# Instance normalisation on one core: mixed PE and bn_stats batches, 4-tile first loads, and small parameter loads moved to another queue

## Chip, cores, metric

One core of one Trainium2 chip runs the whole kernel. The metric is device time in microseconds (us), median of several executions; lower is better. Each execution carries a state, fast or slow. Verdicts use fast runs alone and call a difference under 2% "same". Wherever a ratio is given, it is the mean time of one kernel's fast runs over the mean of the other's fast runs of the same rounds, so it is not quite the ratio of the medians that are quoted.

## The reference

```python
B, C, H, W = 32, 576, 16, 32            # x, g, b in bfloat16
def reference(x, g, b):
    mu = x.mean(axis=(-2, -1), keepdims=True)
    var = ((x - mu) * (x - mu)).mean(axis=(-2, -1), keepdims=True)
    xhat = (x - mu) / jnp.sqrt(var + 1e-5)
    return xhat * g.reshape(1, -1, 1, 1) + b.reshape(1, -1, 1, 1)
```

There are 32 x 576 = 18,432 instances of 512 elements. The kernel lays them out as 144 tiles of 128 instances (one per partition). In bfloat16 that is 18.87 MB in and as much out. Every tile must be read once, have its mean and variance taken, and then be rewritten in place as scale * x + bias.

## The kernel before

A small list scheduler in Python places all the work when the program is built. All 144 tiles stay in SBUF (`xt`), so the sync queue issues all loads first, then the stores as tiles are finished. A tile's statistics come in one of two ways:

- a "D" tile: one `bn_stats` on DVE;
- a "P" tile: PE multiplies by -1/512 times the identity and so folds 512 elements into 64 partial sums, DVE reduces them to the mean, and ACT squares (x - mean) with an accumulated sum.

Tiles are grouped in batches. At the end of a batch a handful of tiny DVE and ACT instructions turn the statistics of all its tiles into `scale` and `bias`. Then "applies", one per tile, run on ACT or POOL, whichever is free.

```python
# [cut: cost table]
head = [("D", 2), ("P", 2), ("D", 4), ("P", 3), ("D", 8), ("P", 5)]   # a batch is all D or all P
tail = [("D", 6), ("P", 3), ("D", 4)]                                 # between them 14 D, 8 P, ...
# [cut: load_chunks: 2, 2, 4 tiles, then 8 tiles each]
@block.sync
def _(sp):
    em = _Emit(sp, None, "SP")
    for ci, (a, e_) in enumerate(load_chunks):
        if ci == plan["gb_after"]:                                    # after the second load
            sp.dma_start(gb4[:, 0, :], g_src).then_inc(sGB, 16)
            sp.dma_start(gb4[:, 1, :], b_src).then_inc(sGB, 16)
        sp.dma_start(xt[:, a:e_, :], xr[:, a:e_, :]).then_inc(ld_sems[ci], 16)
    for s_ in stores:
        dep_waits(em, [("ap", n) for n in range(s_["t0"], s_["t1"])])
        sp.dma_start(outr[:, s_["t0"]:s_["t1"], :], xt[:, s_["t0"]:s_["t1"], :]).then_inc(sST, 16)
    sp.wait_ge(sST, 16 * len(stores))
# [cut: the other engines run the streams that the scheduler made]
```

Of the kernel before, what the change touches and what calls it, by code (L numbers as in the profile page):

```python
# [2 lines left out]

# [12 lines left out]
EPS = 1e-5  # L16

COST = dict(
    bn=593.0,
    sq=704.0,  # L20
    mm=240.0,
    mm_fixed=150.0,
    ap_A=705.0,
    ap_G=744.0,
    ap_V=325.0,
    small=90.0,
    small_per_elem=1.05,
    rd_fixed=130.0,
    rd_per_tile=67.0,
    sqrt=110.0,  # L30
    lat=130.0,
    tile_dma=306.0,
    dma_start=1050.0,
    dma_fixed=40.0,
    dma_issue=450.0,
# [3 lines left out]
class _Task:  # L39
    __slots__ = ("key", "eng", "dur", "deps", "cls", "order", "batch", "start", "end", "idx", "ready", "idx_sq")  # L40

    def __init__(self, key, eng, dur, deps, cls, order, batch=None):
        self.key = key
        self.eng = eng
        self.dur = dur
        self.deps = deps
        self.cls = cls
        self.order = order
        self.batch = batch
        self.start = None  # L50
        self.end = None
        self.idx = None
        self.ready = None


def _default_pattern(nt):
    if nt < 24:
        pat = []
        left = nt
        typ = "D"  # L60
        while left > 0:
            s = min(left, 3 if typ == "D" else 2)
            pat.append((typ, s))
            left -= s
            typ = "P" if typ == "D" else "D"
        return pat
    head = [("D", 2), ("P", 2), ("D", 4), ("P", 3), ("D", 8), ("P", 5)]
    tail = [("D", 6), ("P", 3), ("D", 4)]
    used = sum(s for _, s in head) + sum(s for _, s in tail)
    mid = []  # L70
    left = nt - used
    typ = "D"
    while left > 0:
        s = 14 if typ == "D" else 8
        s = min(s, left)
        mid.append((typ, s))
        left -= s
        typ = "P" if typ == "D" else "D"
    return head + mid + tail


def build_plan(nt, pattern=None, load_chunks=None, cost=None, store_max=8, store_big=16, store_tail=4,
               use_pool=True, use_pe=True):
# [5 lines left out]
    if not use_pe:  # L89
        pattern = [("D", s) for _, s in pattern]  # L90
    assert sum(s for _, s in pattern) == nt, (pattern, nt)
    batches = []
    t0 = 0
    for typ, s in pattern:
        assert typ in ("D", "P")
        if typ == "P":
            assert s <= 8, "P batch must fit one PSUM bank (8 tiles)"
        batches.append(dict(typ=typ, t0=t0, t1=t0 + s, idx=len(batches)))
        t0 += s
    tile_batch = [None] * nt  # L100
    for b in batches:
        for n in range(b["t0"], b["t1"]):
            tile_batch[n] = b["idx"]

    if load_chunks is None:
        load_chunks = []
        sizes = [2, 2, 4]
        pos = 0
        for s in sizes:
            if pos + s <= nt:  # L110
                load_chunks.append((pos, pos + s))
                pos += s
        while pos < nt:
            s = min(8, nt - pos)
            load_chunks.append((pos, pos + s))
            pos += s
    assert load_chunks[0][0] == 0 and load_chunks[-1][1] == nt
    tile_chunk = [None] * nt
    arrive = []
    t = c["dma_start"]  # L120
    n_issue = 0
    gb_after = min(2, len(load_chunks))
    for ci, (a, b_) in enumerate(load_chunks):
        if ci == gb_after:
            n_issue += 2
            t += 100.0
        t = max(t, n_issue * c["dma_issue"] + c["dma_start"])
        n_issue += 1
        t += (b_ - a) * c["tile_dma"] + c["dma_fixed"]
        arrive.append(t)  # L130
        for n in range(a, b_):
            tile_chunk[n] = ci
    gb_arrive = (gb_after + 2) * c["dma_issue"] + c["dma_start"] + 400.0
# [11 lines left out]
    add(("SQ0",), "A", 1400.0, [("DS",)], -1)  # L145
    add(("I0",), "G", 350.0, [], -1)
    add(("I0s",), "G", 200.0, [], -1)
    add(("I1",), "V", 100.0, [("I0",)], -1)
    add(("I1s",), "V", 100.0, [("I0s",)], -1)
    add(("GB",), "T", 300.0, [("I1s",), ("gbld",)], -1)  # L150

    psum_banks = 4
    p_batches = [b for b in batches if b["typ"] == "P"]
    for k, b in enumerate(p_batches):
        b["bank"] = k % psum_banks
        b["pk"] = k
    junk_n = 4
    sq_list = []
    for b in batches:
        bi = b["idx"]  # L160
        w = b["t1"] - b["t0"]
        sm = c["small"] + c["small_per_elem"] * w
        if b["typ"] == "D":
            for n in range(b["t0"], b["t1"]):
                add(("bn", n), "V", c["bn"], [("ld", tile_chunk[n])], 10, bi)
            last_bn = [("bn", n) for n in range(b["t0"], b["t1"])]
            add(("R1", bi), "V", sm, last_bn, 1, bi)
            add(("R2a", bi), "V", sm, last_bn, 1, bi)
            add(("R2b", bi), "V", sm, last_bn, 1, bi)
            add(("T2", bi), "V", sm, [("R2a", bi), ("R2b", bi)], 1, bi)  # L170
            add(("V", bi), "V", sm, [("T2", bi), ("R1", bi)], 1, bi)
            add(("C1", bi), "A", c["sqrt"], [("V", bi)], 0, bi)
            ms_dep = ("R1", bi)
        else:
            deps = [("ld", ci) for ci in sorted(set(tile_chunk[n] for n in range(b["t0"], b["t1"])))] + [("I1",)]
            if b["pk"] >= psum_banks:
                deps.append(("Rd", p_batches[b["pk"] - psum_banks]["idx"]))
            add(("mm", bi), "T", c["mm_fixed"] + c["mm"] * w, deps, 10, bi)
            add(("Rd", bi), "V", c["rd_fixed"] + c["rd_per_tile"] * w, [("mm", bi)], 1, bi)
            add(("Cp", bi), "V", sm, [("Rd", bi)], 2, bi)  # L180
            for n in range(b["t0"], b["t1"]):
                deps = [("Rd", bi)]
                if len(sq_list) >= junk_n:
                    deps.append(("sq", sq_list[-junk_n]))
                tsq = add(("sq", n), "A", c["sq"], deps, 10, bi)
                tsq.idx_sq = len(sq_list)
                sq_list.append(n)
            add(("C1", bi), "A", c["sqrt"], [("sq", n) for n in range(b["t0"], b["t1"])], 0, bi)
            ms_dep = ("Cp", bi)
        add(("C2", bi), "V", sm + 25, [("C1", bi)], 0, bi)  # L190
        add(("C3", bi), "V", sm, [("C2", bi), ("GB",)], 0, bi)
        add(("C4", bi), "V", sm, [("C3", bi), ms_dep], 0, bi)
        add(("C5", bi), "V", sm, [("C4", bi), ("GB",)], 0, bi)
# [22 lines left out]
    ap_dur = dict(A=c["ap_A"], G=c["ap_G"], V=c["ap_V"])  # L216
    v_drain = [False]
    g_stop = [False]
# [17 lines left out]
    def pick(eng, t):  # L236
# [15 lines left out]
        if soon is not None and eng in ("V", "A"):  # L252
            starving = ap_backlog(t) <= 2
            if starving and soon - t <= 450.0:
# [3 lines left out]
        can_apply = (eng == "A") or (eng == "G" and use_pool and not g_stop[0]) or (eng == "V" and not pending["V"])  # L258
# [8 lines left out]
    while n_left > 0:  # L267
        guard += 1
        assert guard < 200000, "scheduler stuck"
        progressed = False  # L270
        for eng in sorted(engines, key=lambda e: free[e]):
# [7 lines left out]
            if tk.key[0] == "ap":  # L279
                ap_pending.remove(tk)  # L280
                tk.eng = eng
                tk.dur = ap_dur[eng]
                if eng == "V":
                    g_stop[0] = True
# [28 lines left out]
    while a < nt:  # L313
# [5 lines left out]
        else:  # L319
            sz = store_big if ap_end[min(nt - 1, a + store_big - 1)] < arrive[-1] else store_max  # L320
# [5 lines left out]
    tq = arrive[-1]  # L326
    slack = []
    for s in stores:
        slack.append(tq - (s["ready"] + 600.0))
        tq = max(tq, s["ready"] + 600.0) + (s["t1"] - s["t0"]) * c["tile_dma"] + c["dma_fixed"]  # L330
    makespan = max(tk.end for tk in tasks.values())
    return dict(
        nt=nt, batches=batches, load_chunks=load_chunks, stores=stores, tasks=tasks, streams=streams,
        tile_batch=tile_batch, tile_chunk=tile_chunk, makespan=makespan, est_total=tq + 2000.0,
        junk_n=junk_n, psum_banks=psum_banks, cost=c, use_pool=use_pool, gb_after=gb_after,
        store_slack=slack,
    )


def plan_summary(plan):  # L340
# [9 lines left out]
    lines.append(f"  compute makespan {plan['makespan']/1e3:.1f}us  est total {plan['est_total']/1e3:.1f}us")  # L350
# [22 lines left out]
def bass_standalone__instancenorm__sampling_kernel(  # L373
# [26 lines left out]
    have_p = any(bb["typ"] == "P" for bb in batches)  # L400
# [6 lines left out]
    with nc.Block() as block, contextlib.ExitStack() as es:  # L407
# [11 lines left out]
        rstd_sb = sb("rstd_sb", [P, NT], F32)  # L419
        t_sb = sb("t_sb", [P, NT], F32)  # L420
        st = sb("st", [P, NT, 6], F32)
        d_sb = sb("d_sb", [P, NT], F32)
        q_sb = sb("q_sb", [P, NT], F32)
        v_sb = sb("v_sb", [P, NT], F32)
        std_sb = sb("std_sb", [P, NT], F32)
        nm_sb = sb("nm_sb", [P, NT], F32)
# [8 lines left out]
        assert NT * 2 + NT <= 512 and 3 * NT <= 512  # L435
        MA_ps = ps[:, 4, 0:2 * NT].rearrange("p (n j) -> p n j", j=2)
        d_ps = ps[:, 4, 2 * NT:3 * NT]
        nm_ps = ps[:, 5, 0:NT]
# [4 lines left out]
        HALF = float(F // 4)  # L443

        def dep_waits(em, deps):
            need = {}
            for d in deps:
                if d[0] == "ld":
                    sem, val = ld_sems[d[1]], 16
                elif d[0] == "gbld":  # L450
                    sem, val = sGB, 32
                else:
                    pt = tasks[d]
                    sem, val = sem_of[pt.eng], pt.idx + 1
# [170 lines left out]
```

## Time and profile before

| | before |
|---|---|
| median, first 4 runs | 96.58 us (96.28 to 96.64) |
| span of the profiled run | 94.8 us |
| bytes moved | 37.79 MB |
| DVE / ACT / POOL busy | 82% / 79% / 73% |
| batches | 19 |

The first view is the page of the kernel before. In the rows of 40, each column is a slice of 2.37 us; DMA is the busy share in tenths and GB/s what moved in that slice. The last line is the summary, by engine, of the chain of work that ended last.

```profile
span 94.8 us, 749 instructions
...
DMA  1899999999999999999999999999999999779996
GB/s 35 240 379 425 425 425 429 432 415 429 415 422 425 411 429 425 418 425 422 415 467 436 415 415 415 429 453 429 404 429 422 418 436 425 321 297 442 404 401 245
...
q1 hardware_dynamic: 5200, 37.75, 96.2%
...
ACT 53%; DMA 20%; SPq 6%; issue 5%; DVE 4%; PE 4%; DVEq 1%
...
```

What to see: the DMA row is full (9) almost everywhere, at 404 to 467 GB/s. Less moves in the first three slices (35, 240, 379), in slices 35 and 36 (321, 297), and in the last. The chain names ACT for 53%. That is the chain of compute; it matters only where a store is late because of it.

The second view gives the same kernel in stretches: from:to in us, length, busy time of each engine with its number of instructions, granted PE clock, DMA share, GB/s.

```profile
...
core 0: us, PE busy (x) PEld busy (x) DVE busy (x) ACT busy (x) POOL busy (x), PEclk, DMA share, GB/s
...
3.50:4.00 0.50, 0.00 (x0) 0.00 (x0) 0.36 (x1) 0.00 (x0) 0.00 (x0) 1.00 0.96 156
4.00:4.50 0.50, 0.24 (x3) 0.24 (x4) 0.50 (x2) 0.00 (x0) 0.00 (x0) 1.00 0.45 57
4.50:5.00 0.50, 0.50 (x8) 0.50 (x5) 0.47 (x2) 0.00 (x0) 0.00 (x0) 1.00 0.75 229
60.00:70.00 10.00, 0.00 (x0) 0.00 (x0) 10.00 (x28) 10.00 (x16) 10.00 (x14) 0.50 1.01 427
...
82.00:83.00 1.00, 0.00 (x0) 0.00 (x0) 1.00 (x4) 1.00 (x3) 1.00 (x3) 0.50 0.45 188
83.00:84.00 1.00, 0.00 (x0) 0.00 (x0) 1.00 (x10) 1.00 (x4) 1.00 (x2) 0.50 0.41 172
84.00:85.00 1.00, 0.00 (x0) 0.00 (x0) 0.42 (x4) 1.00 (x3) 1.00 (x2) 0.50 0.95 401
...
```

Two holes: 3.5 to 5 us (156, 57, 229 GB/s) and 82 to 84 us (188, 172). The steady rate is 427. The waits of the sync queue after 78 us say what the second hole was waiting for, and the timeline shows how late the last coefficients come (start, length, instruction):

```profile
...
engine line waited for: us in total, times, longest us
SPq L370 <- POOL xt L555: 6.0, 2, 4.2
...
```

```profile
...
84.54 2.91 ACT L552 ACTIVATE xt<-xt,bias_sb,scale_sb 128x512 bf16<-128x512 bf16 x4
...
85.28 0.16 DVE L534 TENSOR_TENSOR bias_sb<-ps,t_sb 128x4 f32<-128x4 f32 x1
...
```

The store queue waited once for 4.2 us for an apply of POOL. The last `bias` is written at 85.3 us, and ACT begins its last four applies at 84.5 us.

### The profile page before, as it was taken

Reading aid. Unit: us, or ns where it says so; the run is one execution under the profiler, and the core shown is the slowest. Engines: PE = TensorE matmul, PEld = TensorE weight load, DVE = VectorE, ACT = ScalarE, POOL = GpSimd, SP = SyncE. Lnnn points to the kernel's source line nnn. Section 1 sums busy time; section 2 is a strip of 40 time slices with the busy share of each in tenths; the row PEclk is TensorE's granted clock in tenths of the full one; section 3 lists DMA queues with packets and bytes.
Section 4 is the critical chain, followed back from the end, with each engine's and each line's share of the span. In section 5 each row is a group of like instructions: output and inputs, shape, how many; then the busy total and the mean of one; then the engine's idle time right before and its main releaser. Section 6 shows DMA issues by size and latency. Waiting matters only on the chain.

```text
span 94.8 us, 749 instructions
## 1 busy us (share of the span) xinstructions
PE 23.1 (24%) x74; PEld 9.2 (10%) x74; DVE 77.3 (82%) x245; ACT 75.1 (79%) x171; POOL 68.8 (73%) x96
## 2 busy tenths in 40 slices
PE   0230554039129209494087000000000000000000
PEld 0210431013013003030044000000000000000000
DVE  2445687997899999999899998999999988979000
ACT  6062575959699499999999999999999999999000
POOL 3000600989992399999999999999999999995000
PEclk9999999999999999999955555555555555555555
DMA  1899999999999999999999999999999999779996
GB/s 35 240 379 425 425 425 429 432 415 429 415 422 425 411 429 425 418 425 422 415 467 436 415 415 415 429 453 429 404 429 422 418 436 425 321 297 442 404 401 245
DMA packets 5204, 37.79 MB, mean 399 GB/s; under 512 B 592, under 2 KB 592, under 8 KB 1232
## 3 DMA queue, kind: packets, MB, share of 16 engines
q1 hardware_dynamic: 5200, 37.75, 96.2%
q14 instruction: 4, 0.03, 0.1%
HBM read 18.88 MB, written 18.87 MB: 398 GB/s over the span
## 4 chain that ended last, share of the span: by engine, by line
ACT 53%; DMA 20%; SPq 6%; issue 5%; DVE 4%; PE 4%; DVEq 1%
ACT xt L552 29%; ACT junk L538 22%; DMA xt<-in_x_dram 20%; SPq L574 5%; PE ps L547 4%; DVE xt L555 2%; ACT std_sb L518 1%; DVE nm_sb L512 1%; DVEq L407 1%; DVE rstd_sb L521 0%; SPq L572 0%; DVE t_sb L529 0%; DVE scale_sb L524 0%; DVE bias_sb L534 0%; SPq L573 0%
## 5 line engine op out<-in xcount | busy, mean ns | idle before, releaser
L555 POOL TENSOR_SCALAR xt<-xt,scale_sb,bias_sb 128x512 bf16<-128x512 bf16 x90 | 67.9, 781 | 17.3 <-DVE bias_sb L534 8.9
L491 DVE BATCH_NORM_STATS2 st<-xt 128x6 f32<-128x512 bf16 x94 | 60.0, 679 | 4.0 <-DMA xt<-in_x_dram 4.0
L538 ACT ACTIVATE junk<-xt,nm_sb 128x512 bf16<-128x512 bf16 x50 | 35.4, 710 | 8.3 <-DVE nm_sb L512 8.3
L552 ACT ACTIVATE xt<-xt,bias_sb,scale_sb 128x512 bf16<-128x512 bf16 x50 | 36.6, 803 | 2.2 <-DVE bias_sb L534 2.1
L547 PE MATMUL ps<-xt,ident 128*128 128x512 bf16 (+3 forms) x72 | 22.8, 496 | 28.5 <-DMA xt<-in_x_dram 16.7
L547 PEld LDWEIGHTS ps<-xt,ident 128*128 128x128 bf16 x72 | 9.0, 139 | 41.9 <-issue 26.7
L538 ACT ACTIVATION_READ_ACCUMULATOR junk<-xt,nm_sb 128x1 f32 x50 | 9.5, 189 | 0.0
L512 DVE TENSOR_REDUCE nm_sb<-ps 128x8 f32<-128x512 f32 (+3 forms) x9 | 4.6, 514 | 2.3 <-PE ps L547 2.1
L521 DVE RECIPROCAL rstd_sb<-std_sb 128x8 f32<-128x8 f32 (+6 forms) x19 | 3.7, 194 | 2.1 <-ACT std_sb L518 2.1
L518 ACT ACTIVATE std_sb<-v_sb 128x8 f32<-128x8 f32 (+6 forms) x19 | 3.7, 199 | 1.2 <-DVE v_sb L506 1.1
L534 DVE TENSOR_TENSOR bias_sb<-ps,t_sb 128x8 f32<-128x8 f32 (+6 forms) x19 | 2.9, 158 | 0.2
L524 DVE TENSOR_TENSOR scale_sb<-ps,rstd_sb 128x8 f32<-128x8 f32 (+6 forms) x19 | 2.9, 156 | 0.2
L555 DVE TENSOR_SCALAR xt<-xt,scale_sb,bias_sb 128x512 bf16<-128x512 bf16 x4 | 2.2, 598 | 0.0
L494 DVE TENSOR_REDUCE ps<-st 128x28 f32<-128x56 f32 (+4 forms) x10 | 1.9, 189 | 0.1
L488 ACT ACT_TABLE_LOAD x1 | 1.3, 1283 | 0.7 <-PEq L610 0.7
L529 DVE SCALAR_TENSOR_TENSOR t_sb<-ps,scale_sb 128x14 f32<-128x14 f32 (+4 forms) x10 | 1.6, 162 | 0.2
L500 DVE TENSOR_REDUCE ps<-st 128x14 f32<-128x28 f32 (+4 forms) x10 | 1.8, 175 | 0.0
L497 DVE TENSOR_REDUCE d_sb<-st 128x14 f32<-128x28 f32 (+4 forms) x10 | 1.7, 168 | 0.0
L503 DVE SCALAR_TENSOR_TENSOR q_sb<-d_sb,ps 128x14 f32<-128x14 f32 (+4 forms) x10 | 1.5, 153 | 0.0
L506 DVE TENSOR_TENSOR v_sb<-q_sb,ps 128x14 f32<-128x14 f32 (+4 forms) x10 | 1.5, 151 | 0.0
L515 DVE COPY ps<-nm_sb 128x8 f32<-128x8 f32 (+3 forms) x9 | 1.4, 160 | 0.0
L531 DVE TENSOR_TENSOR t_sb<-ps,scale_sb 128x8 f32<-128x8 f32 (+3 forms) x9 | 1.3, 149 | 0.1
(14 smaller groups left out, 2.9 us busy)
## 6 DMA issues: line engine op xcount, KB each, us to landing
xt<-in_x_dram SPq DMA_DIRECT2D x17, 1024.0 KB, 22.5
out_dram<-xt SPq DMA_DIRECT2D x11, 1024.0 KB, 6.5
out_dram<-xt SPq DMA_DIRECT2D x3, 2048.0 KB, 17.6
out_dram<-xt SPq DMA_DIRECT2D x2, 512.0 KB, 6.0
xt<-in_x_dram SPq DMA_DIRECT2D x2, 256.0 KB, 3.0
xt<-in_x_dram SPq DMA_DIRECT2D x1, 512.0 KB, 5.6
gb<-in_g_dram SPq DMA_DIRECT2D x1, 1.1 KB
gb<-in_b_dram SPq DMA_DIRECT2D x1, 1.1 KB
```

The source lines that it names most:

```text
L491: ins = e.bn_stats(st[:, n, :], xt[:, n, :])
L494: ins = e.tensor_reduce(MA_ps[:, t0:t1, :], st_pairs(t0, t1 - t0, 1, 2), AX.X, ALU.add)
L512: ins = e.tensor_reduce(nm_sb[:, t0:t1], src, AX.X, ALU.add)
L518: ins = e.activation(std_sb[:, t0:t1], v_sb[:, t0:t1], ACTF.Sqrt, bias=EPS, scale=1.0 / F)
L521: ins = e.reciprocal(rstd_sb[:, t0:t1], std_sb[:, t0:t1])
L524: ins = e.tensor_tensor(scale_sb[:, t0:t1], g_ps[:, t0:t1], rstd_sb[:, t0:t1], ALU.mult)
L534: ins = e.tensor_tensor(bias_sb[:, t0:t1], b_ps[:, t0:t1], t_sb[:, t0:t1], ALU.add)
L538: ins = e.activation(junk[:, j, :], xt[:, n, :], ACTF.Square, bias=nm_sb[:, n:n + 1], scale=1.0, accum_out=v_sb[:, n:n + 1])
L547: ins = e.matmul(dst, ident[:], xt[:, t0:t1, j * NP_:(j + 1) * NP_], start=(j == 0), stop=(j == JB - 1), skip_group_check=True)
L552: ins = e.activation(xt[:, n, :], xt[:, n, :], ACTF.Identity, bias=bias_sb[:, n:n + 1], scale=scale_sb[:, n:n + 1])
L555: ins = e.tensor_scalar(xt[:, n, :], xt[:, n, :], scale_sb[:, n:n + 1], bias_sb[:, n:n + 1], ALU.mult, ALU.add)
L574: sp.dma_start(xt[:, a:e_, :], xr[:, a:e_, :]).then_inc(ld_sems[ci], 16)
```

## The change

The intent is to bring the kernel nearer to its DMA limit. Batches become mixed: each has some P and some D tiles and one set of coefficient instructions, so there are 7 batches instead of 19. The first loads are 4 tiles instead of 2. The loads of g and b (1.1 KB each) move from the sync queue to ACT's queue. The last applies no longer go to DVE. The scheduler's cost table is set anew, and a factor of 2 or 4 moves between the statistics instructions so that both kinds of tile share one set.

```diff
+_TUNED_PATTERNS = {
+    144: [(5, 9), (7, 7), (12, 14), (8, 15), (10, 19), (4, 16), (2, 16)],   # (P tiles, D tiles) per batch
+}
-    head = [("D", 2), ("P", 2), ("D", 4), ("P", 3), ("D", 8), ("P", 5)]
-    tail = [("D", 6), ("P", 3), ("D", 4)]
...
-        sizes = [2, 2, 4]
+        load_sizes = [4, 4] + [8] * ((nt - 8) // 8 + 1)
...
         @block.sync
             for ci, (a, e_) in enumerate(load_chunks):
-                if ci == plan["gb_after"]:
-                    sp.dma_start(gb4[:, 0, :], g_src).then_inc(sGB, 16)
-                    sp.dma_start(gb4[:, 1, :], b_src).then_inc(sGB, 16)
                 sp.dma_start(xt[:, a:e_, :], xr[:, a:e_, :]).then_inc(ld_sems[ci], 16)
...
         @block.scalar
+            a.dma_start(gb4[:, 0, :], g_src).then_inc(sGB, 16)
+            a.dma_start(gb4[:, 1, :], b_src).then_inc(sGB, 16)
...  (cost table, coefficient arithmetic and bookkeeping of waits left out)
```

## The prediction

> What bounds it now. The DMA engines. The page gives 37.79 MB for a 94.8 us span; in the slices from 7 us to 80 us they are 90% busy or more and move about 425 GB/s. The Trainium skill ("DMA: Bandwidth & Descriptors", Bandwidth) measured 425 GB/s for one core's 16 MB copy; this trace agrees, so I take 425 as the ceiling. 37.75 MB at 425 GB/s is 88.8 us. First bytes move at 1.8 us and the span ends 1 us after the last byte, so the floor is near 91.6 us; 3.2 us are lost. The stretches of the trace show where:
> - Start: between 3.5 and 5.0 us the rate falls to 156, 57, 229 GB/s. The sync queue issued two 256 KB loads, then the tiny g and b loads (0.37 and 0.26 us), then the next. To 10 us 1.5 us is missing, some of it ramp.
> - 82 to 84 us: 188 and 172 GB/s, about 1.15 us lost. The last store queue waited for POOL's applies (one wait of 4.2 us): the tail batches' coefficients came late, and DVE has no slack after 40 us.
> - After 84 us the rate is about 405, some 0.4 us.
> The chain of waits names ACT 53%, but ACT matters only where it makes a store late.
>
> What changes. (1) First loads 512 KB instead of 256 KB; g and b move to ACT's queue, so x loads are issued about 0.43 us apart with nothing between. (2) 19 batches (10 by bn_stats, 9 by PE) become 7 mixed ones: 96 bn_stats (was 94), 48 squares (was 50). Small DVE instructions fall from about 150 to 70; at 0.10 us each DVE saves about 7 us. PE reductions, 0.64 us for 8 tiles, are 10 instead of 9. (3) The applies: POOL 92 (was 90), ACT 52 (50), DVE none (4). The new scheduler costs only reorder.
>
> Timeline by hand from trace paces (bn 0.597, square 0.704, ACT apply 0.704, POOL apply 0.755 us): first load lands about 4.2, second 5.5, third 8.0. The first batch now needs 9 bn up to tile 13, so first coefficients come near 14.5 us (was 9.2). POOL then runs nearly without gaps: 92 x 0.755 = 69.5, ending near 84 to 86 (was 86.7). DVE: 57 bn + 4.6 PE reductions + 8 small + 2.5 waits from 5.5 gives last coefficients near 78 to 79 (was 85.4). The last 18 tiles are split 9 and 9, ready near 85.8. DMA by then has moved only about 35.8 of 37.75 MB, so stores are queued ahead: no starvation in the tail, slack of 2 to 3 us. First stores need only be ready at 46 us.
>
> So: start saves about 1.0 to 1.3, the dip at 82 to 84 saves 1.1, the tail 0.2 to 0.5; together near 2.8.
>
> Predicted: 93.8 us, 8 in 10 between 93.0 and 95.2; faster by over 2% 0.80, within 2% 0.18, slower 0.02.
>
> To check: no slice under 400 GB/s between 5 and 88 us; no fall at 3.5 to 5 us; POOL first apply near 14.5 us, last coefficients near 79, last apply near 86; DVE idle grows; the chain ends in DMA, not ACT.
>
> What would make it wrong: the fall at 3.5 us is ramp or latency of the queue, not the g and b loads (then 94.8); a batch boundary leaves POOL and ACT idle and the stores starve mid-way (95 or more); stores drain slower than 425 at the end.

## The result, and the profile after

The changed kernel took 95.01 us (median of 11 runs, 94.79 to 95.22), the kernel before 96.35 us (median of 16). The ratio is 0.985 (95% interval 0.9824 to 0.9875): within 2%, though clearly faster. Executions over 1.5% slower than the fastest of the same kernel are left out of the means. The time lies inside the predicted range, near its slow end. The gain is half of the 2.8 us that was forecast, and the likeliest class (faster by over 2%, at 0.80) did not come.

The page of the changed kernel, the same lines (a slice is now 2.32 us):

```profile
span 92.8 us, 678 instructions
...
DMA  2999999999999999999999999999999999999993
GB/s 34 362 445 420 431 424 424 424 424 420 427 413 424 416 424 420 424 416 427 409 455 452 431 424 395 431 427 424 420 431 431 427 427 431 424 424 427 434 406 152
...
q1 hardware_dynamic: 5184, 37.75, 97.5%
...
POOL 74%; DVE 7%; DMA 5%; PE 2%; POOLq 1%; issue 0%; SPq 0%
...
```

The same stretches of the changed kernel:

```profile
...
core 0: us, PE busy (x) PEld busy (x) DVE busy (x) ACT busy (x) POOL busy (x), PEclk, DMA share, GB/s
...
3.50:4.00 0.50, 0.00 (x0) 0.00 (x0) 0.00 (x0) 0.00 (x0) 0.00 (x0) 1.00 1.11 437
4.00:4.50 0.50, 0.00 (x0) 0.00 (x0) 0.00 (x0) 0.00 (x0) 0.00 (x0) 1.00 1.01 418
4.50:5.00 0.50, 0.40 (x2) 0.13 (x2) 0.00 (x0) 0.00 (x0) 0.00 (x0) 1.00 1.11 459
60.00:70.00 10.00, 0.00 (x0) 0.00 (x0) 10.00 (x26) 10.00 (x16) 10.00 (x14) 0.50 1.01 426
...
82.00:83.00 1.00, 0.00 (x0) 0.00 (x0) 0.00 (x0) 1.00 (x3) 1.00 (x2) 0.50 1.01 426
83.00:84.00 1.00, 0.00 (x0) 0.00 (x0) 0.00 (x0) 0.52 (x1) 0.99 (x2) 0.50 1.01 426
84.00:85.00 1.00, 0.00 (x0) 0.00 (x0) 0.00 (x0) 0.00 (x0) 0.00 (x0) 0.50 0.99 418
...
```

Both holes are gone. From the third slice on, the queue runs at 409 to 455 GB/s, with one slice at 395, until the last two (406, 152). Compute has become early: the timelines below give the last `bias` and the last ACT applies, then POOL's applies.

```profile
...
75.68 7.84 ACT L593 ACTIVATE xt<-xt,bias_sb,scale_sb 128x512 bf16<-128x512 bf16 x11
...
76.40 0.18 DVE L577 TENSOR_TENSOR bias_sb<-ps,t_sb 128x18 f32<-128x18 f32 x1
```

```profile
...
14.72 69.27 POOL L596 TENSOR_SCALAR xt<-xt,scale_sb,bias_sb 128x512 bf16<-128x512 bf16 x92 [13.21 <-DVE bias_sb L577]
```

The last coefficients come at 76.4 us (85.3 before), ACT's last applies end at 83.5 and POOL's at 84.0 us, and POOL runs 92 applies without a gap. After 84 us only the queue works, for 8 us. So nearly everything that the prediction asked of the profile is there. The question is why it buys only half. One check needs a warning: I had said that the chain would end in DMA. The page's chain says POOL 74%. That chain follows the last piece of compute; experiment 1 shows that the time does not depend on it.

### A finer reading: the completions of one transfer

On the sync queue, the changed kernel has 576 packets of 4 bytes for its 36 loads and stores, 16 for each. The Trainium skill ("DMA: Bandwidth & Descriptors", Why a DMA increments its semaphore by 16 and not by 1) says that a DMA runs on up to 16 engines that finish independently, and that each posts its own increment after its data. So the 16 four-byte packets of the last store show when each of the 16 DMA engines was done. That each comes from another engine is the page's statement; the trace agrees in the count. The packed records do not name the engine of a packet, so which engine is late cannot be read here. In the table, times are from the first data packet (about 1.7 us into the span), counted from the packet records of each profiled execution; "mean" is over the 16. Where the engines lie further apart than the last store takes (1.25 us), the last 16 packets can hold two of one engine; in the rows from a 1.6 us spread up this sets the mean up to 0.13 us too late.

```
profiled run   time    mean of 16  last of 16  last - first  time - last
before         96.60     92.18       92.28        0.18          4.32
after          94.88     89.70       90.38        1.07          4.50
a_nowait       95.15     89.79       90.68        1.25          4.47
a_gb_late      95.23     89.76       90.72        1.29          4.51
a_oldstart     96.05     90.58       91.53        1.32          4.52
a_gb_sp        95.89     90.52       91.37        1.39          4.52
b_nowait       96.23     90.66       91.96        1.81          4.27
b_newstart     96.12     91.67       91.77        0.18          4.35
b_gb_act       96.45     92.05       92.14        0.17          4.31
a_bigst        95.37     89.84       90.88        1.62          4.49
a_big          95.34     89.44       90.81        1.70          4.53
a_pe6          95.99     90.05       91.31        1.94          4.68
a_pad          96.18     89.90       91.69        2.46          4.49
```

The first two rows account for the result. The average DMA engine finished 2.48 us earlier (92.18 - 89.70), close to the 2.8 predicted. The last one finished only 1.90 us earlier (92.28 - 90.38), because the engines now finish 1.07 us apart instead of 0.18. Another 0.18 us went between the last completion and the end of the time (4.50 against 4.32). 2.48 - 0.58 - 0.18 = 1.72 us, which is 96.60 - 94.88. In all 13 rows the time follows the last engine, by 4.27 to 4.68 us.

Following the spread from transfer to transfer shows where it comes from. In the kernel before, the completions of one transfer were about 2.0 us apart from the third load (7.6 us) on, stayed so until the store that ended at 84.0 us, and were 0.16 us apart at the next one: the hole at 82 to 84 us is where the engines that were ahead ran dry and waited, while the late ones worked off their queue. The last completion of the transfer before the hole came at 83.97 us of the span and that of the next at 86.44, 2.47 us later. One engine's share of such a transfer is 8 packets of 309 ns, 2.47 us: the latest engine had no idle time to lose in that hole. In the changed kernel they were 0.47 us apart from 5 to 25 us, 1.08 at the load ending at 28.1 us, and stayed at 1.07 to the end, since nothing made the early engines wait.

That leads to the theory and its rivals:

- Theory A: the changed kernel is bound by the queue of its latest DMA engine; in the kernel before, the latest engine's queue and the end of compute were two bounds of nearly equal length, so the hole at 82 to 84 us cost almost nothing.
- Rival B: the hole was a plain loss of 1.1 us (the prediction), and something else in the changed kernel, a compute wait, takes it back.
- Rival C: the gain comes from one part of the change alone, the start or the batches.

### The profile page after: what moved, and what is told of

The parts are those of the page before. It is cut to its first block, busy times and chain, and to the rows that moved or that the text cites. A ratio compares the mean times of both kernels' runs of the same rounds, so it can differ in the third digit from the quotient of the medians.

```text
span 92.8 us, 678 instructions
## 1 busy us (share of the span) xinstructions
PE 21.4 (23%) x74; PEld 9.0 (10%) x74; DVE 69.8 (75%) x178; ACT 73.5 (79%) x157; POOL 70.1 (76%) x98
## 4 chain that ended last, share of the span: by engine, by line
POOL 74%; DVE 7%; DMA 5%; PE 2%; POOLq 1%; issue 0%; SPq 0%
POOL xt L596 74%; DMA xt<-in_x_dram 5%; DVE st L551 4%; PE ps L588 2%; DVE ma_sb L567 1%; POOLq L470 1%; SPq L612 0%; DVE ma_sb L553 0%; DVE scale_sb L573 0%; DVE v_sb L561 0%; DVE rstd_sb L571 0%; DVE ps L559 0%; DVE ps L557 0%; DVE bias_sb L577 0%; DVE d_sb L555 0%
## 5 line engine op out<-in xcount | busy, mean ns | idle before, releaser
L596 POOL TENSOR_SCALAR xt<-xt,scale_sb,bias_sb 128x512 bf16<-128x512 bf16 x92 | 69.3, 769 | 13.2 <-DVE bias_sb L577 13.2
L581 ACT ACTIVATE junk<-xt,ma_sb 128x512 bf16<-128x512 bf16 x48 | 33.9, 707 | 7.1 <-DVE ma_sb L567 7.1
L588 PE MATMUL ps<-xt,ident 128*128 128x512 bf16 (+4 forms) x72 | 21.0, 474 | 18.7 <-DMA xt<-in_x_dram 18.7
L581 ACT ACTIVATION_READ_ACCUMULATOR junk<-xt,ma_sb 128x1 f32 x48 | 9.0, 187 | 0.0
L567 DVE TENSOR_REDUCE ma_sb<-ps 128x8 f32<-128x512 f32 (+4 forms) x9 | 4.5, 502 | 1.2 <-PE ps L588 1.2
L569 ACT ACTIVATE std_sb<-v_sb 128x14 f32<-128x14 f32 (+5 forms) x7 | 1.5, 214 | 1.4 <-DVE v_sb L561 1.2
L571 DVE RECIPROCAL rstd_sb<-std_sb 128x14 f32<-128x14 f32 (+5 forms) x7 | 1.9, 269 | 0.3 <-ACT std_sb L569 0.3
L553 DVE TENSOR_REDUCE ma_sb<-st 128x32 f32<-128x64 f32 (+5 forms) x7 | 1.4, 200 | 0.1
L557 DVE TENSOR_REDUCE ps<-st 128x16 f32<-128x32 f32 (+5 forms) x7 | 1.3, 188 | 0.0
L555 DVE TENSOR_REDUCE d_sb<-st 128x16 f32<-128x32 f32 (+5 forms) x7 | 1.3, 180 | 0.0
```

Source lines behind the costliest of these rows:

```text
L553: ins = e.tensor_reduce(ma_sb[:, tm:t1, :], st_pairs(tm, t1 - tm, 1, 2), AX.X, ALU.add, negate=True)
L555: ins = e.tensor_reduce(d_sb[:, tm:t1], st_pairs(tm, t1 - tm, 1, 1), AX.X, ALU.subtract)
L557: ins = e.tensor_reduce(d_ps[:, tm:t1], st_pairs(tm, t1 - tm, 1, 1), AX.X, ALU.subtract)
L567: ins = e.tensor_reduce(ma_sb[:, g0:g1, 0], src, AX.X, ALU.add)
L569: ins = e.activation(std_sb[:, t0:t1], v_sb[:, t0:t1], ACTF.Sqrt, bias=EPS, scale=0.25 / F)
L571: ins = e.reciprocal(rstd_sb[:, t0:t1], std_sb[:, t0:t1])
```

## The experiments

Twelve kernels were run, each with 5 timed rounds beside the kernel before, four at a time on one chip. "a_" kernels start from the changed one, "b_" kernels from the one before. A difference between two of the ratios is uncertain by 0.35 us or more (intervals of 0.25% and more each), and the changed kernel itself was measured in other calls than experiments 1 to 8; the kernels nearest to it in those calls, a_nowait (0.9882) and a_gb_late (0.9861), lie 0.3 and 0.1 us above its 0.985.

### 1. The changed kernel with no store waiting for compute (a_nowait)

Stores wait only for their loads; applies write to scratch, so the result is wrong, while all compute still runs.

```diff
-                dep_waits(em, [("ap", n) for n in range(s_["t0"], s_["t1"])])
+                sp.wait_ge(ld_sems[ci], 16)        # for each load that holds tiles of this store
-                    ins = e.activation(xt[:, n, :], xt[:, n, :], ...)      # tensor_scalar on POOL likewise
+                    ins = e.activation(scrA[:, em.count % 8, :], xt[:, n, :], ...)
```

> Wrong result on purpose: the changed kernel with every store waiting for its loads only, all compute still running but the applies written to scratch. Theory 1 (the changed kernel is bound by its DMA queue alone from first to last byte): the time is that of the changed kernel, 95.0 us within 0.3. Rival (some compute wait still costs): at least 0.7 us faster, 94.3 or less. If Theory 1 holds, the last DMA's 16 completions should again be spread over about 1 us, as in the changed kernel's trace (1.0 us), against 0.18 us in the kernel before.

Measured: 95.15 us (95.07 to 95.26), ratio to before 0.9882. No faster than the changed kernel. Its page:

```profile
span 93.1 us, 676 instructions
...
GB/s 29 358 442 429 429 419 426 422 422 422 422 415 419 419 419 426 419 426 419 426 426 440 450 450 377 436 415 436 419 433 426 426 433 422 422 433 426 433 403 114
...
POOL 69%; DVE 7%; DMA 5%; issue 5%; PE 2%; POOLq 1%; SPq 0%
...
```

The chain still reads POOL 69%, in a kernel whose stores do not wait for POOL at all: a reminder of what that view can say. Taking away the compute waits of the stores bought nothing, so the second half of rival B falls. The completions were 1.25 us apart, as expected.

### 2. The kernel before with no store waiting for compute (b_nowait)

The same edit in the kernel before; again wrong.

> Wrong result on purpose: the kernel before, each store waiting for its loads only, applies written to scratch. The starved stretch of 82 to 84 us goes. If it was a loss for the whole queue (my prediction): 95.0 to 95.2 us, 1.1 less than before. If it mostly was the early DMA engines waiting for the latest one (the completions of one transfer were 2.0 us apart before that stretch and 0.16 us after it): 95.7 to 96.2, and the last transfer's completions end 1.2 to 2 us apart.

Measured: 96.24 us (95.75 to 96.34), ratio 0.9976 (0.9935 to 1.0017). Three of the stretches:

```profile
...
4.00:4.50 0.50, 0.34 (x4) 0.34 (x5) 0.50 (x2) 0.00 (x0) 0.00 (x0) 1.00 0.67 115
...
82.00:83.00 1.00, 0.00 (x0) 0.00 (x0) 1.00 (x8) 1.00 (x3) 1.00 (x2) 0.50 1.01 426
83.00:84.00 1.00, 0.00 (x0) 0.00 (x0) 0.45 (x6) 1.00 (x4) 1.00 (x2) 0.50 0.99 418
...
```

The hole at 82 to 84 us is filled (426, 418 GB/s, where before there were 188 and 172), and the time does not change beyond noise. In the table, the mean engine finished 1.52 us earlier (92.18 to 90.66), the last one 0.32 us (92.28 to 91.96). This refutes rival B's first half, which is the step of my prediction that credited 1.1 us to the hole. The two profiled runs alone are not a clean pair: in b_nowait the latest engine fell another 0.6 us behind between 61 and 69 us, about an instruction packet at 63.6 us, which it did not in the kernel before. At the hole itself the reading is clean: with the waits the latest engine completed the stores on its two sides at 83.97 and 86.44 us, without them at 83.84 and 86.30.

### 3. New batches, old start (a_oldstart)

```diff
-        load_sizes = [4, 4] + [8] * ((nt - 8) // 8 + 1)
+        load_sizes = [2, 2, 4] + [8] * ((nt - 8) // 8 + 1)
+                if ci == 2:
+                    sp.dma_start(gb4[:, 0, :], g_src).then_inc(sGB, 16)     # and b; both lines go from ACT
```

> New batches, old start (loads of 2, 2, 4 tiles; g and b on the sync queue after the second load). Theory 1 (my prediction: the start's gap is a plain loss, worth 1.0 to 1.3 us, and adds to the rest): 96.0 to 96.3 us, that is 1.0 to 1.3 slower than the changed kernel's 95.0, nearly all of the gain gone. Rival (the gain is that of the tail dip, the start is worth little): 95.0 to 95.5. The stretch 3.5 to 5 us should show the fall to about 60 to 230 GB/s again.

Measured: 95.99 us, ratio 0.996 (0.9934 to 0.9987). DVE, ACT's compute and POOL run the same instructions as in the changed kernel.

```profile
span 94.0 us, 679 instructions
...
GB/s 37 242 396 425 432 425 425 432 411 429 418 418 429 411 429 422 418 418 425 429 464 425 425 418 404 432 422 429 429 425 425 429 425 429 429 425 425 432 404 105
...
```

The start's fall is back (242, 396 in the second and third slices), the hole near 83 us is not, and three quarters of the gain are lost: 0.996 against 0.985 is 1.1% of 96.24 us, or 1.06 us, give or take 0.35. With 425 GB/s as the full rate, the bytes of the first four slices put the start of full flow at 3.32 us here (9.40 us less 2.585 MB / 425 GB/s) and at 2.40 us in the changed kernel (9.28 us less 2.926 MB / 425 GB/s), 0.92 us earlier. (The page counts a packet's bytes at its start; spread over the packets' durations, both come 0.15 us later.) So the start's term of the prediction, 1.0 to 1.3 us, was right in size within the noise, given the new batches.

### 4. Old batches, new start (b_newstart)

```diff
-        sizes = [2, 2, 4]
+        sizes = [4, 4]
-                if ci == plan["gb_after"]:      # both parameter loads go to ACT's queue, as in the change
```

The old scheduler reorders its instructions somewhat for the new load sizes, so this is not the start alone to the letter.

> Old batches with the whole new start (loads 4, 4, 8 tiles; g and b on ACT's queue; the old scheduler reorders its instructions a little for it). Theory 1 (gains of start and batches add; the start alone is worth 1.0): 95.2 to 95.5 us. Theory 2 (the old batches' compute ends near 87 us whatever the loads do, so the start alone buys nothing): 96.0 to 96.6, last apply near 87, and a deeper starved stretch near 80 to 84 us.

Measured: 95.85 us, ratio 0.9945 (0.9906 to 0.9985). Neither theory's number: between them. Two stretches, at the start and at the hole:

```profile
...
4.00:4.50 0.50, 0.00 (x0) 0.00 (x0) 0.00 (x0) 0.00 (x0) 0.00 (x0) 1.00 1.02 418
...
82.00:83.00 1.00, 0.00 (x0) 0.00 (x0) 1.00 (x5) 1.00 (x2) 1.00 (x3) 0.50 0.16 66
...
```

The start flows (418 GB/s at 4 to 4.5 us) as in the changed kernel. In exchange the hole at 82 to 83 us is deeper, 66 GB/s, and the last transfer's completions are 0.18 us apart: the engines that were ahead had run dry and waited for compute. The latest one again did not wait in that hole: its completions before and after it are 2.47 us apart (83.30 and 85.77). It waited about 0.2 us near 90 us, behind POOL's last apply (end 88.5). Compute is close behind it all the same: the first engines started the store after the hole at 83.04 us (85.51 less 2.47), so without its own lateness the latest engine could have won 0.26 us there and no more.

Experiments 1 to 4 together are a table of the two parts, as ratios to before: neither 1; batches alone 0.996; start alone 0.9945; both 0.985. The parts alone gain 0.4% and 0.55%, together 1.5%. That is 0.55% more than the sum, with an uncertainty of about as much (0.54%), and against the later measurement of the changed kernel (0.991, experiment 12) nothing is left of it; so that the parts do not add is suggested, not shown. Rival C falls against the first measurement, whose interval lies clear of both parts'. The reading that fits the traces: with the start alone, compute still ends late; with the batches alone, the latest engine still starts late; only both together shorten the longer of the two bounds.

### 5. Old batches, g and b on ACT's queue, nothing else (b_gb_act)

```diff
-                if ci == plan["gb_after"]:
-                    sp.dma_start(gb4[:, 0, :], g_src).then_inc(sGB, 16)     # and b
+            a.dma_start(gb4[:, 0, :], g_src).then_inc(sGB, 16)             # and b, first on ACT's queue
```

> Old batches, g and b on ACT's queue, nothing else. Theory 1 (gains add): 95.3 to 95.6 us. Theory 2 (the old batches finish late in any case, so bytes moved earlier only lengthen the starved stretch near 82 to 84 us): 96.1 to 96.5 us, and the starved stretch loses about 2 us instead of 1.15. If the loads landing earlier also let DVE start earlier, something between.

Measured: 96.65 us (96.31 to 97.7), ratio 1.0059 (1.0015 to 1.0103): no gain. It agrees with theory 2's "no gain", but it is a weak test: in its profiled run the bytes of the first 10 us hardly rose, because packets between 6 and 9 us were slower than usual, and I have no cause for that. The other half of theory 2 did not come: with 172 and 213 GB/s at 82 to 84 us the starved stretch lost about 1.1 us, as before, not 2. Experiment 4 is the better one.

### 6. The changed kernel with g and b back on the sync queue (a_gb_sp)

Only the place of the two parameter loads differs from the changed kernel; the first loads stay at 4, 4 and 8 tiles.

> The changed kernel with g and b on the sync queue after the second load, loads still of 4, 4, 8 tiles. If the g and b loads themselves made the gap of 3.5 to 5 us (their place in the queue): about 0.8 to 1.2 us slower than 95.0. If the gap came from two small first loads running dry while the queue was busy issuing g and b: the first two loads now hold 2.5 us of data, the issue of g and b takes 0.8, so no slower than 95.1.

Measured: 95.78 us, ratio 0.9946 (0.9919 to 0.9974), about 0.9 us slower than the changed kernel, give or take 0.35. The stretches behind the second load:

```profile
...
core 0: us, PE busy (x) PEld busy (x) DVE busy (x) ACT busy (x) POOL busy (x), PEclk, DMA share, GB/s
...
5.00:5.50 0.50, 0.00 (x0) 0.00 (x0) 0.00 (x0) 0.00 (x0) 0.00 (x0) 1.00 1.04 215
5.50:6.00 0.50, 0.08 (x2) 0.11 (x2) 0.17 (x1) 0.00 (x0) 0.00 (x0) 1.00 0.48 197
...
```

The fall has moved to 5 to 6 us (215, 197 GB/s), behind the now larger first loads, although the third load had been issued at 2.35 us. So the two tiny transfers make the hole by standing in the queue; it is not that small first loads ran dry while they were issued. Load sizes explain little: 0.996 (experiment 3) against 0.9946 here. The Trainium skill ("DMA: Bandwidth & Descriptors", Issuing engines are not separate DMA queues) says that issuing from several engines saves only issue time, since all run on the same 16 engines. The trace shows more here: issuing g and b took 0.63 us on the sync queue (0.37 and 0.26), but that had ended at 2.3 us, long before the flow fell at 5.0, so what they cost is the hole. By 15 us, 0.38 MB less had moved than in the changed kernel (4.92 against 5.30), 0.9 us at 425 GB/s. The times alone do not separate 0.9 from 0.63.

### 7. The changed kernel with g and b issued later on ACT's queue (a_gb_late)

```diff
-            a.dma_start(gb4[:, 0, :], g_src).then_inc(sGB, 16)     # and b, first on ACT's queue
+            if k == "SQ0":                                         # placed behind the table load
+                e.dma_start(gb4[:, 0, :], g_src).then_inc(sGB, 16) # and b
```

> The changed kernel with g and b issued on ACT's queue after the table load (about 3.1 us instead of 0.73). If these two tiny transfers slow the ramp at 1.7 to 2.5 us (82 GB/s there): 94.4 to 94.7. If the ramp is the first load's own latency: 94.8 to 95.2, and the stretch 2.0 to 2.5 us still shows about 80 GB/s.

The edit did less than planned: the trace shows the two issued at 0.91 and 1.49 us, while the table load was still running (0.73 to 2.01 us), not at 3.1. Their packets moved later all the same, at 2.9 to 3.5 and 4.6 to 5.1 us instead of 1.7 and 3.6 to 4.0, so none fell into the slow ramp.

Measured: 95.04 us, ratio 0.9861, with 74 GB/s at 2.0 to 2.5 us. In experiment 6, where g and b moved at 4.9 to 5.1 us, that stretch also shows 74 GB/s. The slow ramp is not due to the packets of g and b. That is the 0.6 us by which I had mis-set the beginning: I took full flow from 1.8 us, and it amounts to 2.40 us.

### 8 and 9. Larger transfers (a_big, a_bigst)

```diff
-        load_sizes = [4, 4] + [8] * ((nt - 8) // 8 + 1)      # a_big only
+        load_sizes = [4, 4, 8] + [16] * 8
-  store_max=8, store_big=16, store_tail=4                    # both
+  store_max=16, store_big=16, store_tail=4
```

> The changed kernel with 16-tile loads after the first three and 16-tile stores. An 8 KB packet took 309 ns and a 16 KB one 611 in the trace, so a packet costs some 7 ns apart from its bytes; one DMA engine's sum falls by about 0.45 us for loads and 0.40 for stores. If the queue of the latest engine is all that bounds the changed kernel: 94.0 to 94.3 us. If compute, which now gets its later loads in larger steps, has no slack: 95 or more, with a slice under 400 GB/s after 50 us.

> The changed kernel with stores of 16 tiles (nine, then 12 and 4), loads and instruction streams untouched. Fewer, larger packets: one DMA engine's sum should fall by 0.40 us (104 packets of 309 ns and 16 of 611 become 64 of 611 and 8 of about 460). If the latest DMA engine bounds the kernel: 94.5 to 94.7, without the 44 to 46 us trouble of the run with 16-tile loads. If stores become late: 95 or more.

(The record's "nine" is a slip: a_bigst has eight stores of 16 tiles, then 12 and 4.)

Measured, fast runs only (each has one slow run, 96.01 and 96.05 us): a_big 95.34 us (94.53 to 95.64), ratio 0.9866 (0.9805 to 0.9927); a_bigst 95.00 us (94.44 to 95.37), ratio 0.9851 (0.9799 to 0.9902). The fastest single runs are theirs, but the medians are no better than the changed kernel's first 95.01 and the fast runs scatter over about 1 us. In a_bigst's own call the unedited changed kernel was slower (experiment 12): means of fast runs 94.97 against 95.54 us. That would be more than the 0.40 us worked out, but the intervals of the two ratios overlap, so it is not shown. In the table a_big's mean engine was indeed the earliest of all (89.44), and its engines were 1.70 us apart, so the last was no earlier.

```profile
span 93.3 us, 654 instructions
...
GB/s 34 368 439 467 429 407 436 450 443 422 422 407 432 446 436 415 414 422 446 323 422 422 429 429 436 443 429 414 443 429 429 436 436 414 443 422 411 441 390 30
...
```

Slice 20 (323 GB/s) is a disturbance in a_big's profiled run where loads give way to stores. Of the 33 packets of 16 KB that began between 44.5 and 46 us, 27 took over 700 ns instead of 611. I did not find its cause. In the mean, the larger packets roughly save what was worked out, but only after other losses are added back: a_big's mean engine ended 0.26 us before the changed kernel's, and slice 20 alone cost about 0.55 us (323 instead of 424 GB/s), together near 0.85; a_bigst's ended 0.14 us after it, having lost about 0.5 us in the first 15 us (5.09 MB against 5.30), so the stores saved about 0.35. The latest engine kept what was saved. There is no established better version in these two.

### 10 to 12. Is an instruction fetch what makes an engine late? (a_pe6, a_pad, after_again)

In the changed kernel's packet records there are three 8 KB packets of the instruction queue inside the span, at 25.6, 31.2 and 39.6 us. The next slow data packet after each took 968, 689 and 659 ns, against 309 for the others, and the spread of the completions rose from 0.47 to 1.08 us just after the first. Three kernels were to test it.

```diff
# a_pe6: fewer PE groups, so a shorter PE stream
-    144: [(5, 9), (7, 7), (12, 14), (8, 15), (10, 19), (4, 16), (2, 16)],
+    144: [(5, 9), (8, 8), (8, 14), (8, 15), (8, 19), (8, 16), (0, 18)],
# a_pad: 56 memsets of an unused tile on POOL, while it waits for its first coefficients
+            if k == "I0s":
+                for i in range(56):
+                    e.memset(pad[:, i:i + 1], 0.0)
# after_again: the changed kernel, unedited
```

> The changed kernel with PE tiles in 6 groups instead of 9 (45 squares, 99 bn_stats), so that PE's stream is short enough to need no second instruction fetch. The trace of the changed kernel shows three 8 KB instruction fetches on the DMA engines (25.6, 31.2, 39.5 us), and the packet after each takes 968, 689, 659 ns instead of 309. If a fetch makes one DMA engine late and the latest one ends the kernel: with the 25.6 us fetch gone, the completions of one transfer are about 0.5 us apart at the end and the time is 94.3 to 94.6; with another one gone, two fetches are left, and the time is 94.7 to 95.1. If fetches do not matter: 95.0 in either case. Compute ends a us later, still ahead of the queue.

> The changed kernel with 56 tiny memsets of an unused tile on POOL, while POOL waits for its first coefficients: POOL's stream becomes long enough for one more instruction fetch. Prediction of the fetch theory: a fourth 8 KB fetch in the trace, one more slow packet behind it; the time rises by 0 to 0.7 us, by how much depends on which DMA engine it hits (none if that one is ahead). If fetches do not matter: 95.0 and no change in the completions' spread.

> The changed kernel itself, unchanged, on the same chip as the other three, for comparison: 95.0 us, three instruction fetches, completions of one transfer about 1.0 to 1.4 us apart at the end.

Measured: a_pe6 95.17 us (95.04 to 95.99), ratio 0.9896; a_pad 95.24 us (94.85 to 96.18), ratio 0.9881; the changed kernel again 95.87 us (94.78 to 95.97, and one slow run of 96.44), ratio 0.991 (0.9854 to 0.9967). Neither edit did what it was made for. a_pe6 still has three fetches (27.0, 29.4, 39.8 us). a_pad has three too (6.6, 26.9, 32.0 us): the one near 40 us was replaced by an early one, where I had expected a fourth. So these two do not test the theory, and the three intervals overlap.

What this did show is scatter. On this chip the fast runs of the unedited changed kernel ran from 94.78 to 95.97 us. In the profiled runs of all three (after_again's is slow), the early packets between 4.5 and 8 us were slow, and the completions at the third load were already 1.5 to 1.7 us apart. In a_pad's profiled run (96.18 us) the spread went from 1.54 to 2.48 us just after its fetch at 26.9 us, while its mean engine (89.90) was as early as the changed kernel's (89.70); the 1.3 us between those two times are the last engine's (91.69 against 90.38). In a_pe6 the fetch at 27.0 us left the spread as it was (1.33); it then grew from 1.35 to 1.97 us between 48 and 88 us with no fetch in that time, so a fetch is not the only thing that makes an engine late.

The other traces add to this. Just after the first fetch, with the same slow packet of 968 or 969 ns behind it, the spread rises in a_nowait (0.76 to 1.34), a_gb_late (0.51 to 1.35), a_oldstart (0.71 to 1.36), a_gb_sp (1.03 to 1.36) and b_newstart (0.77 to 1.58); it does not in the kernel before (2.03) and in b_nowait (1.39), where the engines were already far apart. If the fetch (332 ns) and the slow packet (659 ns too long) are on one engine, that engine loses 0.99 us, enough for each of these rises. A rise in some runs and none in others is what one expects if a fetch delays one engine, which is sometimes the latest; but no run here takes a fetch away, so that is argued, not shown.

## Why the prediction was right, and where it was not

1. The bound. "The DMA engines", with 425 GB/s as ceiling: right. The changed kernel moves 425 GB/s on end, as the Trainium skill's figure for a 16 MB copy says ("DMA: Bandwidth & Descriptors", Bandwidth), and taking away every wait for compute leaves it at 95.15 us (experiment 1).
2. The start, "about 1.0 to 1.3" us: right in size and cause, 1.06 us between experiment 3 and the changed kernel (give or take 0.35; 0.92 by the start of full flow), and g and b standing in the sync queue are most of it (experiment 6). With the old batches the new start gave only 0.55% (experiment 4).
3. "The dip at 82 to 84 saves 1.1": this is the step that failed. Filling that hole in the kernel before gained 0.2%, within noise (experiment 2). The rate in the hole is an average over 16 DMA engines. Those ahead waited; the latest one, 2.0 us behind the first, lost nothing in it (83.97 to 86.44 us is one transfer's 2.47), and it sets the end.
4. "The tail 0.2 to 0.5" and "the floor is near 91.6 us" of span: too good. The floor took full flow from 1.8 us, and the ramp makes that 2.40 us; and it let all engines end together, while the last ended 0.68 us after the mean (90.38 - 89.70). The span was 92.8 us.
5. The timeline by hand was good where it mattered: first coefficients and first POOL apply near 14.5 us (measured 14.7), POOL without gaps, last coefficients 78 to 79 (76.4), last apply 84 to 86 (84.0), a slack of 2 to 3 us or better. Later first coefficients indeed cost nothing.
6. The sum, 2.8 us, was right for the mean engine (2.48) and wrong for the last one (1.90); a further 0.18 us was given back after the last completion. That the time still fell into the stated range, 93.0 to 95.2, is partly luck: the range was wide enough for a gain of half the size, but none of the three reasons given for such a gain was the one that came.

What stays open: why one engine falls behind in the first 8 us, and by how much in which run; whether instruction fetches are the cause of the later step; whether the two parts of the change add; why the changed kernel spends 4.5 us outside its transfers where the old one spends 4.3; and why the last chip scattered more. Since the fast runs of after_again straddle those of the first measurement (0.991 against 0.985), the size of the gain itself depends somewhat on chip and execution.

## What to carry to other kernels

A hole in the DMA rate is a loss only if the DMA engine that ends last was idle in it: compare the 16 completions of one transfer before and after the hole, and take the waits away in a throwaway version before crediting the bytes. Two bounds of nearly equal length (the last engine's queue and the end of compute) hide each other, so parts of a change tested singly may each look worth less than they are; here that is just at the edge of the noise. Keep tiny transfers out of the queue that carries the bulk, at least near its start, the only place tested here.

## What the Trainium skill lacked or had wrong

- "DMA: Bandwidth & Descriptors": it says that the engines of one transfer finish independently, but gives no figure for how far apart they end or for how long. Here one transfer's completions were 0.5 to 2.5 us apart for most of a run, and the last engine ended 0.7 to 1.8 us after the mean in the runs that no wait for compute had brought together.
- "DMA: Bandwidth & Descriptors", Issuing engines are not separate DMA queues: issuing elsewhere is said to save only issue time. Two 1.1 KB loads standing in the bulk queue cost 0.9 us, give or take 0.35 (experiment 6), in a hole at 5 to 6 us; their issue, 0.63 us, had ended at 2.3 us.
- "Runtime: NRT & Kernel Launch", Instruction fetch mechanics: it calls the cost of crossing a block of instructions "mostly hidden". For POOL's stream no wait shows (it runs from 14.7 to 84.0 us without a gap); but each fetch appears here as an 8 KB packet on the DMA engines, and a data packet right behind it took 659 to 968 ns instead of 309. The page's blocks are 16 KiB; the packets here have 8 KB.
- "DMA: Bandwidth & Descriptors", Specifications, gives about 0.6 us to the first byte for a load issued from the sync queue, but not from when it counts. Here 1.0 us pass from the start of the first issue to the first data (0.73 to 1.7 us) and 0.6 us from its end (1.1 us), so only the second agrees. No page gives the ramp after it, which costs 0.7 us more (full flow from 2.40 us).
